# Agent attention into a top-1 mixture of experts: the second layer in 128 columns, gated out of its bank, single banks, another order of loads, left tiles by batch

## The chip, the cores and the metric

The kernel runs on one core of one Trainium2 chip. The metric is the device time of one execution in microseconds. A core has five engines that matter here, each working through its own list of instructions in order: PE (TensorE, matmuls, with its weight loads shown apart as PEld), DVE (VectorE), ACT (ScalarE), POOL (GpSimd) and SP (SyncE, which issues most of the DMA transfers). An engine that reaches an instruction whose operand is not there waits, and all that is queued behind it on that engine waits too.

## The reference

Four batches of N = 11456 tokens with C = 128 channels. The first function is agent attention (49 agents), the second a mixture of 8 experts with F = 1024 hidden units, of which each token takes the one with the largest logit.

```python
def _attn_ref(q, k, v, agents):
    scale = 1.0 / np.sqrt(q.shape[-1])
    def sm(a, b):                       # softmax of scale * a b^T
        ...
    a2k = sm(agents, k)
    agent_v = a2k @ v
    q2a = sm(q, agents)
    return (q2a @ agent_v).astype(np.float32)

def _moe_ref(x, w_gate, w_output_gate, w1, w2):
    logits = x @ w_gate
    e_idx = np.argmax(logits, axis=1)
    ...
    gate_w = probs[np.arange(N), e_idx]
    eom = 1.0 / (1.0 + np.exp(-(x @ w_output_gate)))
    for e in range(E):
        mask = e_idx == e
        ...
        h = np.maximum(x[mask] @ w1[e], 0.0)
        ye = h @ w2[e]
        out[mask] = gate_w[mask, None] * eom[mask, e, None] * ye
```

## The kernel before

The tokens of a batch are cut into 12 units of 1024 (the last has 192). A unit of k passes `k_unit` (scores tile ks, copied to S, maximum mx), a unit of v passes `v_unit` (exponentials ev, sums av), and a unit of q passes `q_unit` (scores qs) and `q_rest`, which makes the softmax over the agents in two 16-bit parts, turns it by a DMA into x1 (tile x_ld in the profile), and computes gate logits lg and the tests t. What the attention gives for a token is a mix of 49 agent vectors, so that x @ w1 is x1 times a small matrix made once per batch.

This matrix is made by a chain of steps between the batches. `fold(b)` sums the agents' values (av from sel); `choose` finds the expert that most tokens of the batch take and loads its w1 and w2; `units`, `split_units`, `signs`, `linear` and `second` build the weights of the first layer (tiles awp, kr, pm, wp), those of the part that is linear (lin) and those of the second layer (vp, vv); `gates` builds those of the logits. Each of these is a few small operations on PE, DVE, ACT and POOL in turn. Hidden units whose sign is the same for all tokens of the batch go into lin, so that NK = 2 blocks of 128 hidden units remain.

The main stream (`main_stream`) has 92 tiles, 23 per batch, of four token tiles of 128 tokens each (the last of a batch has two of 96). `mm1` makes h = x1 times the first layer in a pair of banks of 2 x 512 columns of PSUM; `relu` makes the high 16-bit part hh on ACT and the low one hl on DVE; `mm2` makes y for one token tile from five matmuls: x1 with lin (256 columns: 128 with the high part of the weights, 128 with the low part), and for each of the two blocks hh with vv (256 columns) and hl with the high part of vv (128 columns). The columns of high and low parts stand side by side, so that two token tiles fill a bank. `finish` copies a bank to ys on ACT (ring of two), adds the two halves into os on POOL (ring of four), and `store` multiplies os by the gate factor of the tokens, smt, and sends it out. The factor smt is made by `route` for a group of three units at once, that is for six main tiles.

Tokens whose expert is not the batch's are left to a second path: `q_tail` counts them, `left_table` makes a table of tiles of up to 128 tokens of one expert, `left_index` computes indices and gathers the rows (tile big), and `left_static` computes each such tile with the expert's whole weights (let, lx, lh, ly) and `left_scatter` writes its rows over those of the main stream. PHASES names the batches of a table and the tiles that are computed in any case: batches 0 to 2 have one table with 16 tiles, batch 3 one with 3. A loop at the end, on a count read on the chip, covers what that does not hold; its body does not run with these inputs.

The order of all instructions is made when the kernel is built. The class Clock keeps an estimate of the time at which each engine gets to each instruction; `spawn` adds a generator with a priority to a list; `tick`, `block` and `idle` are called by the main stream between its matmuls, and each steps those generators whose next instruction would not have to wait by that estimate. `order()` is a list of all k, v and q units and says in which order they are loaded (SP issues) and scored; `AHEAD` bounds how many q units may be ahead of the main stream, `RING` how many tiles of hh and hl there are. PSUM has eight banks: four stand as two pairs for h and t, four are single.

## Time and profile before

| | |
|---|---|
| median of three runs (lowest to highest) | 931.98 us (928.88 to 932.38) |
| the profiled execution, its span, the rest | 932.74 us, 930.9 us, 1.8 us |
| mean granted clock of TensorE | 0.828 |
| busy over the span: PE, PEld, DVE, ACT, POOL | 76%, 58%, 64%, 44%, 45% |
| startup, until the first h | 83.4 us |
| main tiles of batch 0, 1, 2, 3 | 148.6, 133.9, 130.0, 170.8 us |
| between them | 61.4, 51.3, 48.4 us |
| after the last y | 103.1 us |

The stages were cut where the first h and the last y of each batch stand in PE's timeline. A row of stages gives, for each stretch, the busy time of each engine with its number of instructions, the clock that TensorE was granted as a share of 2.4 GHz, the busy share of the DMA engines and what they moved. A row of a group gives what an operation writes and reads, its shape, how often it ran, its busy time and the mean of one, and then the idle time of its engine just before it and who ended it. Matmuls overlap, so their own durations say little; the distance from one start to the next is what a matmul takes of PE.

### The profile page before, as it was taken

The page shows a single profiled execution, that of the slowest core. Times are in us where ns is not written, and L with a number is a line of the kernel's source. Part 1 is how long each engine was busy: PE and PEld are TensorE (multiplying, and loading weights), DVE is VectorE, ACT ScalarE, POOL GpSimd, SP SyncE. Part 2 cuts the span into 40 slices and gives each one's busy share as a digit, 9 for nine tenths or more (in the row PEclk, how much of TensorE's full clock was granted, in tenths as well). Part 3 has the DMA queues.
Part 4 walks back from the last instruction along what each step waited for, and adds up shares of the span by engine and source line. Part 5 has one row for each costly group of instructions (what it writes and reads, how often), then busy time and mean ns, then how long its engine had stood idle before and what let it go on. Part 6 is the DMA issues. An engine that isn't in the chain of part 4 may idle for free. (4 is left out here: it accounts for less than half of the span.)

```text
span 930.9 us, 22198 instructions
## 1 busy us (share of the span) xinstructions
PE 705.7 (76%) x8709; PEld 537.6 (58%) x8709; DVE 597.5 (64%) x1346; ACT 412.0 (44%) x836; POOL 415.1 (45%) x658
## 2 busy tenths in 40 slices
PE   9989768778637986968579869653876859898765
PEld 7777636556525754747456647451544637677654
DVE  2666678676745975867659868688784668663310
ACT  2353626454342653635435636444343435452221
POOL 3110427756300475655104956651237555673331
PEclk9999978997757977977579879775887869898787
DMA  9962565565951447749914577482004715549440
GB/s 326 314 225 72 175 118 168 145 196 163 282 151 39 142 153 188 199 132 211 263 52 139 166 197 206 139 251 46 7 20 149 146 53 160 168 148 297 138 134 27
DMA packets 105081, 146.75 MB, mean 158 GB/s; under 512 B 60477, under 2 KB 69425, under 8 KB 104972
## 3 DMA queue, kind: packets, MB, share of 16 engines
q1 hardware_dynamic: 103148, 143.18, 53.0%
q0 software_dynamic: 1824, 2.11, 1.1%
q8 instruction: 69, 1.13, 0.5%
q14 instruction: 40, 0.33, 0.1%
HBM read 96.79 MB, written 35.50 MB: 142 GB/s over the span
## 5 line engine op out<-in xcount | busy, mean ns | idle before, releaser
L223 POOL TENSOR_TENSOR os<-ys 128x256 f32<-128x256 f32 x180 | 133.8, 753 | 161.6 <-ACT ys L223 114.4
L223 PE MATMUL y<-vv,hh 128*128 128x256 f16 x720 | 180.7, 292 | 0.0
L223 PEld LDWEIGHTS <-x_ld 128*128 128x128 f16 (+1 forms) x1080 | 96.8, 108 | 106.0 <-issue 49.1
L223 ACT COPY ys<-y 128x512 f32<-128x512 f32 x180 | 103.7, 585 | 121.1 <-POOL os L223 66.1
L223 PE MATMUL y<-lin,x_ld 128*128 128x256 f16 x360 | 105.6, 293 | 64.6 <-ACT ys L223 44.0
L223 PE MATMUL y<-vv,hl 128*128 128x128 f16 x720 | 152.1, 231 | 0.0
L223 DVE SCALAR_TENSOR_TENSOR hl<-h,hh 128x1024 f16<-128x1024 f32 (+1 forms) x92 | 108.7, 1189 | 40.7 <-ACT hh L223 40.0
L223 ACT ACTIVATE hh<-h 128x1024 f16<-128x1024 f32 (+1 forms) x92 | 91.7, 1000 | 87.8 <-PE h L223 86.1
L223 DVE TENSOR_REDUCE tm<-t 128x4 f32<-128x1024 f32 (+1 forms) x92 | 108.8, 1196 | 32.4 <-PE t L223 31.3
L223 PE MATMUL h<-x_ld,w 128*128 128x512 f16 (+3 forms) x368 | 94.4, 398 | 14.3 <-DVE tm L223 5.5
L223 PEld LDWEIGHTS <-hh 128*128 128x128 f16 x720 | 75.2, 104 | 51.0 <-issue 44.5
L223 PE MATMUL t<-w,x_ld 128*128 128x256 f16 x360 | 77.4, 310 | 6.4 <-DVE hl L223 3.6
L223 PEld LDWEIGHTS <-hl 128*128 128x128 f16 x720 | 75.7, 105 | 6.9
L223 DVE TENSOR_TENSOR os<-os,smt 128x512 f32<-128x512 f32 (+1 forms) x61 | 44.9, 751 | 32.4 <-POOL os L223 27.6
L223 PE MATMUL ks<-at,k_ld 128*64 128x50 f32 (+1 forms) x1636 | 57.7, 233 | 4.1 <-DVE r L223 1.4
L223 PE MATMUL av<-v_ld,ev 128*64 128x129 f32 x720 | 51.2, 286 | 12.6 <-ACT ys L223 12.3
L223 PEld LDWEIGHTS ks<-at,k_ld 128*64 128x64 f32 (+1 forms) x1636 | 51.0, 143 | 12.0 <-issue 4.4
L223 PEld LDWEIGHTS <-w 128*128 128x128 f16 (+1 forms) x368 | 24.7, 96 | 56.6 <-issue 54.4
L223 PE MATMUL lh<-lxs,lw_ld 128*128 128x128 f32 x304 | 54.0, 310 | 4.1 <-ACT lxs L223 2.1
L223 PE MATMUL lg<-gs,x_ld 128*128 128x36 f16 x360 | 31.0, 192 | 33.6 <-DMA x_ld<-e 28.8
L223 PE MATMUL qs<-at,q_ld 128*32 128x50 f32 (+1 forms) x2124 | 50.7, 222 | 3.3 <-issue 2.1
L223 PEld LDWEIGHTS av<-v_ld,ev 128*64 128x64 f32 x720 | 40.5, 140 | 21.0 <-ACT ys L223 14.0
(292 smaller groups left out, 1380.2 us busy)
## 6 DMA issues: line engine op xcount, KB each, us to landing
v_ld<-v SPq DMA_DIRECT2D x44, 516.0 KB
q_ld<-qT SPq DMA_DIRECT2D x44, 512.0 KB
out<-os SPq DMA_DIRECT2D x88, 256.0 KB
k_ld<-kT SPq DMA_DIRECT2D x43, 512.0 KB
lw_ld<-w SPq DMA_DIRECT2D x38, 512.0 KB
efd<-ef SPq DMA_DIRECT2D x44, 200.0 KB
w1t<-w SPq DMA_DIRECT2D x4, 512.0 KB
w2t<-w SPq DMA_DIRECT2D x4, 512.0 KB
```

The source lines that it names most:

```text
L223: return getattr(self.eng, op)(*a, **k)
```

## The change

Five things are changed together.

- `mm2` makes y of a token tile from eight matmuls of 128 columns instead of five: lin in its high part and, for the first 49 rows, in its low part; hh with both parts of vv one after the other; hl as before. All of them go to the same 128 columns, so high and low parts are summed in PSUM, and the four token tiles of a main tile stand in one bank.
- `finish` takes the bank straight to os. Where the factor smt is there (by the order), DVE multiplies it in, or ACT in four instructions of 128 columns; where it isn't, ACT copies and POOL multiplies later (`late`). Over the program DVE does this for 15 tiles, ACT with the factor for 32, and ACT without it for 45. The rings ys and the POOL additions are gone; os still has four places, and a tile waits until the tile four before it is stored.
- PSUM is eight single banks. h takes two, relu runs on each by itself (hh on ACT, hl in `low` on DVE), and the tests t are made for two token tiles at a time.
- `order()` loads k of batch b+2 from four units before the end of batch b and v of batch b+1 earlier in batch b; eight k units of batch 1 are scored before the first main tile instead of three. RING is 4 (was 5), AHEAD 7 (was 5), SMALL 10 (was 8), and `block` has no quiet time after a gather.
- PHASES has a table for each batch with 10, 6, 1 and 4 tiles; the tables, the gathers and the tiles run as generators beside the main stream, with whatever place is free (`left_home`).

```diff
-LARGE, SMALL, KEEP = 7, 8, 3
-PHASES = [(0, 3, 16, 384), (3, 1, 3, 128)]
+LARGE, SMALL, KEEP = 7, 10, 3
+PHASES = [(0, 1, 10, 128), (1, 1, 6, 128), (2, 1, 1, 128), (3, 1, 4, 128)]
...
-    PAIRS = 2
-    banks = [[True, None] for _ in range(6)]
+    banks = [[True, None] for _ in range(8)]
...
-        for h in range(0, nt, 4):
-            n = min(4, nt - h)
-            yield from wait_pair()
-            t = pair(f"t{b}_{u}_{h}")
+        for h in range(0, nt, 2):
+            n = min(2, nt - h)
+            yield from wait_free()
+            t = bank(f"t{b}_{u}_{h}")
             mark = hold()
...
+        rest = [("k", 1, u) for u in range(PRE, NU)]
+        for g in range(2, B * NU):
+            b, u = divmod(g, NU)
+            items.append(("q", b, u))
+            if b == 0 and rest:
+                items += rest[:2]
+                del rest[:2]
+            if u >= NU - LEAD:
+                kb, k0 = b + 2, 2 * (u - NU + LEAD)
             else:
-                items += qs
+                kb, k0 = b + 1, 2 * (LEAD + u)
+            if 1 < kb < B and k0 < NU:
+                items += [("k", kb, k0), ("k", kb, k0 + 1)]
+            v0 = 2 * (u - (6 - LEAD))
+            if b == 0:
+                v0 -= 2 * ((NU - PRE) // 2 + 2 - (6 - LEAD)) if PRE < NU else 0
+            if b + 1 < B and 0 <= v0 < NU:
+                items += [("v", b + 1, v0), ("v", b + 1, v0 + 1)]
...
-    PRE = 6
+    LEAD = 4
+    PRE = 8
...
-    MIX0 = [(2, 0)] + [(1, 0)] * 4 + [(0, 0)] + [(0, 2)] * 6
-    MIX = [(3, 0)] * 4 + [(0, 0)] + [(0, 2)] * 6 + [(0, 0)]
...
-    EARLY = 3
+    EARLY = 8
...
-    RING = 5
+    RING = 4
...
-        p = pair(f"h{i}")
-        mark = hold()
+        p = []
         for g in range(NK):
-            PE.matmul(p[:, g, 0:w], own_[:, g * P:(g + 1) * P], x1, start=True, stop=False)
+            p.append((bank(f"h{i}_{g}"), hold()))
+        for g in range(NK):
+            PE.matmul(p[g][0][:, 0:w], own_[:, g * P:(g + 1) * P], x1, start=True, stop=False)
...
-        spawn(relu(i, p, mark), 0)
...
+        for g, (x, mark) in enumerate(p):
+            yield from ACT.q.activation(hh[:, g, 0:w], x[:, 0:w], AF.Relu)
+            spawn(low(x, hh[:, g, 0:w], hl[:, g, 0:w], mark, i), 0)
+
+    cut = [0] * NT
+
+    def low(x, hh, hl, mark, i):
+        yield from DVE.q.scalar_tensor_tensor(hl, x[:, 0:hl.shape[1]], 0.0, hh, op0=ALU.max, op1=ALU.subtract)
+        release(mark)
+        cut[i] += 1
 
...
         b, u, h, pp, n = tiles[i]
-        k, j = t // 2, t % 2
-        if j == 0:
-            Y[i, k] = bank(f"y{i}_{k}"), hold()
+        if t == 0:
+            Y[i] = bank(f"y{i}"), hold()
         x1, lin = X1[b, u][0], state[b]["lin"]
         hh, hl = H[i] if t + 1 < n else H.pop(i)
         vv = state[b]["vv"]
-        y = Y[i, k][0][0:pp, j * 2 * C:(j + 1) * 2 * C]
+        y = Y[i][0][0:pp, t * C:(t + 1) * C]
         sl = slice(t * pp, (t + 1) * pp)
-        PE.matmul(y, x1[:, (4 * h + t) * pp:(4 * h + t + 1) * pp], lin, start=(j == 0), stop=False)
+        xs = x1[:, (4 * h + t) * pp:(4 * h + t + 1) * pp]
+        PE.matmul(y, xs, lin[:, 0:C], start=(t == 0), stop=False)
+        PE.matmul(y, xs[0:A], lin[0:A, C:2 * C], start=False, stop=False)
         tick()
         for g in range(NK):
-            PE.matmul(y, hh[:, g, sl], vv[:, g].rearrange("p h c -> p (h c)"), start=False, stop=False)
+            PE.matmul(y, hh[:, g, sl], vv[:, g, 0, :], start=False, stop=False)
+            PE.matmul(y, hh[:, g, sl], vv[:, g, 1, :], start=False, stop=False)
             tick()
-            PE.matmul(y[:, 0:C], hl[:, g, sl], vv[:, g, 0, :], start=False, stop=(g == NK - 1 and j == 1))
+            PE.matmul(y, hl[:, g, sl], vv[:, g, 0, :], start=False, stop=(g == NK - 1 and t == n - 1))
...
+        if t == n - 1:
+            if 4 * h + n == UNITS[u][2]:
+                scored(("x1", b, u))
+            spawn(finish(i), 0)
...
+    def finish(i):
         b, u, h, pp, n = tiles[i]
...
+        while i > 3 and i - 4 not in done or ended[0] < i:
+            yield None
+        os = wk.tile([P, 4, C], F32, name=f"os{i}", tag="os", bufs=4)
+        y, mark = Y.pop(i)
+        yv = y[0:pp, 0:n * C].rearrange("p (t c) -> p t c", c=C)
+        ended[0] = i + 1
+        if (b, u) not in SM:
+            yield from ACT.q.copy(os[0:pp, 0:n, :], yv)
+            release(mark)
+            spawn(late(i, os))
+            return
+        smt = SM[b, u][0:pp, 4 * h:4 * h + n]
+        if clk.vt["DVE"] <= clk.vt["ACT"]:
+            yield from DVE.q.tensor_tensor(os[0:pp, 0:n, :], yv, smt.unsqueeze(2).broadcast_to([pp, n, C]), op=ALU.mult)
+        else:
+            for t in range(n):
+                yield from ACT.q.activation(os[0:pp, t, :], yv[:, t, :], AF.Copy, scale=smt[:, t:t + 1])
+        release(mark)
+        yield from store(i, os)
...
+    def late(i, os):
+        b, u, h, pp, n = tiles[i]
+        while (b, u) not in SM:
+            yield None
+        smt = SM[b, u][0:pp, 4 * h:4 * h + n]
+        yield from POOL.q.tensor_tensor(os[0:pp, 0:n, :], os[0:pp, 0:n, :],
+                                        smt.unsqueeze(2).broadcast_to([pp, n, C]), op=ALU.mult)
+        yield from store(i, os)
...
-            if m1 < NT and m1 + 1 - freed <= RING and pair_free() is not None and pair_free()[0] <= now + 20.0:
+            if m1 < NT and m1 + 1 - freed <= RING and frees(2):
...
-            if i in H and "lin" in st and "vv" in st and clk.at([H[i][1], st["vv"], st["lin"]]) <= now:
-                can2 = t % 2 > 0 or n_free() > 0
+            if i in H and cut[i] == NK and "lin" in st and "vv" in st and clk.at([H[i][1], st["vv"], st["lin"]]) <= now:
+                can2 = t > 0 or n_free() > 0
...
+    left_todo = [(ph, k) for ph, x in enumerate(PHASES) for k in range(x[2])]
...
+    def left_tables():
+
+        for ph, (b0, nb, nst, _) in enumerate(PHASES):
+            while counted[0] < b0 + nb:
+                yield None
+            yield from left_table(ph)
...
+    def left_prepare():
+
+        for ph, (b0, nb, nst, _) in enumerate(PHASES):
+            while ph not in tables:
+                yield None
+            for i in range(0, nst, NSTM):
+                n = min(NSTM, nst - i)
+                while left_home() is None:
                     yield None
...
-    AHEAD = 5
+    AHEAD = 7
```

PE, batch 0: one token tile of the second layer, as far as its first block. `x10_..._ld` is the turned softmax, `lin0` and `vv0` are the weights of batch 0, the number behind y, hh and hl is that of the main tile. Before (tile 22):

```order
L223 LDWEIGHTS hl21_3567
L223 MATMUL y21_1_3665<-vv0_1560,hl21_3567 128x128
L223 LDWEIGHTS x10_11_ld_3363
L223 MATMUL y22_0_3686<-lin0_98,x10_11_ld_3363 96x256
L223 LDWEIGHTS hh22_3631
L223 MATMUL y22_0_3686<-vv0_1560,hh22_3631 96x256
```

After (tile 17):

```order
L217 LDWEIGHTS w0_1_1670
L217 MATMUL h18_1_3988<-x20_3_ld_3770,w0_1_1670 128x512
L217 LDWEIGHTS x10_8_ld_3219
L217 MATMUL y17_3907<-lin0_98,x10_8_ld_3219 128x128
L217 LDWEIGHTS x10_8_ld_3219
L217 MATMUL y17_3907<-lin0_98,x10_8_ld_3219 128x128
L217 LDWEIGHTS hh17_3805
L217 MATMUL y17_3907<-vv0_1744,hh17_3805 128x128
L217 LDWEIGHTS hh17_3805
L217 MATMUL y17_3907<-vv0_1744,hh17_3805 128x128
```

Each matmul of 256 columns has become two of 128 with a weight load of the same operand before each.

PE, from batch 0 to batch 1. `y22` is the last tile of batch 0, `av1_3804` from `sel` is the fold of batch 1, `qs`, `ks`, `av` with two numbers are units of scores and values, `ga1` the gates. Before:

```order
L223 MATMUL y22_0_3686<-vv0_1560,hh22_3631 96x256
L223 LDWEIGHTS hl22_3632
L223 MATMUL y22_0_3686<-vv0_1560,hl22_3632 96x128
L223 MATMUL qs1_1_3641<-at_74,q1_1_ld_3154 64x50 x16
L223 MATMUL av1_10_3719<-v1_10_ld_3214,ev1_10_3584 64x129 x8
L223 MATMUL av1_11_3735<-v1_11_ld_3262,ev1_11_3646 64x129 x2
L223 MATMUL qs1_2_3758<-at_74,q1_2_ld_3285 64x50 x16
L223 MATMUL ks2_0_3785<-at_74,k2_0_ld_3543 64x50 x16
L223 MATMUL av1_3804<-sel_72,avs1_0_2555 128x50 x2
L223 MATMUL ks2_1_3818<-at_74,k2_1_ld_3580 64x50 x16
L223 MATMUL ks2_2_3844<-at_74,k2_2_ld_3642 64x50 x16
```

After, at the first tiles that stand behind the fold's chain:

```order
L217 MATMUL y17_3907<-vv0_1744,hh17_3805 128x128
L217 LDWEIGHTS hl17_3806
L217 MATMUL y17_3907<-vv0_1744,hl17_3806 128x128
L217 LDWEIGHTS A161_3441
L217 MATMUL wp1_0_4040<-pm1_3499,A161_3441 128x512
L217 LDWEIGHTS A161_3441
L217 MATMUL wp1_0_4040<-pm1_3499,A161_3441 128x512
L217 LDWEIGHTS A161_3441
L217 MATMUL wp1_0_4040<-pm1_3499,A161_3441 128x512
L217 LDWEIGHTS A161_3441
L217 MATMUL wp1_0_4040<-pm1_3499,A161_3441 128x512
```

Before, the fold of batch 1 stands behind y22 and wp1 behind that; now wp1 stands between y17 and y18 of batch 0. The fold itself stands eight tiles earlier, ahead of y10; at the next two batches five (y29 to y33) and seven (y49 to y55) main tiles stand between fold and wp.

ACT, in batch 1: the eviction of tiles 33 and 34. `ev`, `qz`, `ld_`, `eo`, `S3` and `lv` belong to units of attention and gate logits. Before:

```order
L223 COPY avs2_0_5135<-av2_0_5136 128x129
L223 ACTIVATE qz1_6_4964<-ef1_6_4978 128x8x49
L223 ACTIVATE ev2_3_5259<-ev2_3_5259 128x400
L223 ACTIVATE ld_1_3_5213<-ld_1_3_5213 128x192
L223 ACTIVATE qz1_7_5153<-ef1_7_5175 128x8x49
L223 ACTIVATE eo1_3_5300<-ogs1_3_5296 128x24
L223 COPY ys33_0_5324<-y33_0_5214 128x512
L223 COPY ys33_1_5326<-y33_1_5231 128x512
```

After:

```order
L217 COPY lv_0_95<-lg1_7_6206 128x288
L217 ACTIVATE pm2_5866,less2_5865<-kr2_1_6068,nkey2_5848 128x512
L217 ACTIVATE eo1_3_6239<-ogs1_3_6188 128x24
L217 COPY lv_0_95<-lg1_8_6295 128x288
L217 ACTIVATE os33_6345<-y33_6233,smt1_3_6318 128x128 x4
L217 ACTIVATE v162_6354<-w2t2_5549,s22_s_5762 128x4x128 x2
L217 CAST w2_0_6392<-wp2_0_6359 128x512
L217 COPY S3_3_6086<-ks3_4_6408 128x400
L217 ACTIVATE hh34_6450<-h34_0_6433 128x512
L217 ACTIVATE hh34_6450<-h34_1_6434 128x512
```

The two copies of a tile, with POOL's additions of os33 and os34 behind them, have become four multiplications by `smt1_3` straight into os33; `hh` of a tile is two rows instead of one.

## Rows read from the trace of the kernel before

**Rows 1.** Stages: stretch, length, busy of PE, PEld, DVE, ACT, POOL; clock, DMA, GB/s

```profile
0.00:83.40 83.40, 76.87 (x1071) 62.15 (x1071) 43.30 (x132) 30.45 (x73) 15.86 (x53) 0.98 0.72 242
83.40:232.00 148.60, 116.37 (x1745) 84.99 (x1742) 103.63 (x179) 75.73 (x141) 76.70 (x124) 0.87 0.58 162
232.00:293.40 61.40, 32.87 (x416) 25.39 (x416) 34.19 (x117) 21.10 (x53) 13.06 (x23) 0.61 0.61 165
293.40:427.30 133.90, 110.72 (x1587) 81.28 (x1586) 101.24 (x171) 70.45 (x129) 76.23 (x122) 0.87 0.56 163
427.30:478.60 51.30, 31.91 (x392) 26.06 (x392) 34.58 (x113) 21.10 (x54) 12.90 (x24) 0.60 0.74 177
478.60:608.60 130.00, 107.52 (x1587) 78.83 (x1585) 100.83 (x171) 70.27 (x129) 76.97 (x123) 0.89 0.57 168
608.60:657.00 48.40, 23.43 (x214) 17.70 (x213) 38.83 (x140) 18.83 (x50) 12.13 (x23) 0.61 0.50 122
657.00:827.80 170.80, 133.63 (x1252) 97.18 (x1249) 116.19 (x230) 76.34 (x144) 94.53 (x128) 0.84 0.39 109
827.80:930.90 103.10, 72.36 (x465) 64.01 (x465) 24.70 (x97) 27.68 (x67) 36.68 (x42) 0.82 0.47 146
sum 930.90, PE 705.66 PEld 537.58 DVE 597.49 ACT 411.95 POOL 415.06; mean PE 78.41 PEld 59.73 DVE 66.39 ACT 45.77 POOL 46.12
```

**Rows 2.** Timeline of PE, first boundary: start, duration, instruction, idle before

```profile
236.81 0.65 PE L223 MATMUL av<-sel,avs 128*128 128x50 f32 x4
...
282.98 1.01 PE L223 MATMUL wp<-pm,A 128*128 128x512 f16 x2 [10.73 <-DVE pm L223]
...
292.33 0.39 PE L223 MATMUL wp<-pm,R 128*128 128x256 f16 x2
```

**Rows 3.** Waits: engine, what waited, for what; total us, times, longest

```profile
PE y L223 <- ACT ys L223: 44.0, 16, 6.3
...
POOL os L223 <- DMA out<-os: 34.8, 11, 10.2
```

**Rows 4.** Groups by shape: operation, count, busy us, mean ns, idle before

```profile
L223 ACT COPY ys<-y 128x512 f32<-128x512 f32 x176 | 101.4, 585 | 121.1 <-POOL os L223 66.1 <-PE y L223 49.5 <-PE qs L223 2.1
...
L223 DVE TENSOR_TENSOR os<-os,smt 128x512 f32<-128x512 f32 x59 | 42.8, 740 | 28.1 <-POOL os L223 23.3 <-POOL smt L223 4.8
...
L223 DVE SCALAR_TENSOR_TENSOR hl<-h,hh 128x1024 f16<-128x1024 f32 x88 | 106.5, 1218 | 40.3 <-ACT hh L223 39.7 <-issue 0.2
L223 DVE SCALAR_TENSOR_TENSOR hl<-h,hh 128x384 f16<-128x384 f32 x4 | 2.2, 554 | 0.4 <-ACT hh L223 0.3
...
L223 DVE TENSOR_REDUCE tm<-t 128x4 f32<-128x1024 f32 x88 | 106.1, 1219 | 30.2 <-PE t L223 29.2 <-issue 0.8
```

**Rows 5.** Timeline of PE and PEld, one token tile and a run of loads

```profile
352.14 0.28 PE L223 MATMUL y<-lin,x_ld 128*128 128x256 f16 x1
...
352.37 0.22 PE L223 MATMUL y<-vv,hl 128*128 128x128 f16 x1
352.42 0.27 PE L223 MATMUL y<-vv,hh 128*128 128x256 f16 x1
...
352.59 0.27 PE L223 MATMUL y<-lin,x_ld 128*128 128x256 f16 x1
...
352.37 0.10 PEld L223 LDWEIGHTS <-hh 128*128 128x128 f16 x1
...
357.05 0.29 PEld L223 LDWEIGHTS <-x_ld 128*128 128x128 f16 x8 [2.45 <-DMA x_ld<-e]
```

**Rows 6.** The tail: stage of tile ly alone; a DVE step; two of the chain

```profile
827.80:930.90 103.10, 30.13 (x208) 28.36 (x208) 4.78 (x13) 0.82 0.47 146
...
862.11 0.17 DVE L223 TENSOR_TENSOR ppi<-pexc,tot 128x8 f32<-128x8 f32 x1 [1.31 <-PE lh L223]
...
902.30 0.43 PE let L223
...
921.58 0.71 POOL out L223
```

More of the change, by code (lines that the diff above doesn't have):

```diff
@@ L293, in agent_attention_top1_moe @@
     resting = [False]
-    others = list(range(6))
     def n_free():
-        return sum(banks[k][0] for k in others)
+        return sum(x[0] for x in banks)
     def when_free(x):
@@ L333, in idle_bank, with frees @@
         return min(free)[1] if len(free) > 1 and min(free)[0] <= clk.now() - 600.0 else None
-    def pair_free():
-        free = [(when_free(banks[k]), k) for k in range(PAIRS) if banks[k][0]]
-        return min(free) if free else None
-    def wait_pair():
-        while True:
-            x = pair_free()
-            if x is not None and x[0] <= clk.now() + 50.0:
-                return
-            yield None
+    def frees(n):
+        free = sorted(when_free(x) for x in banks if x[0])
+        return len(free) >= n and free[n - 1] <= clk.now() + 20.0
+    KEEP_LONG, KEEP_SHORT = 2, 1
     def wait_free(long=False):
@@ L416, in agent_attention_top1_moe @@
     e16s = []
-    for i in range(4):
+    for i in range(3):
         t = cp.tile([P, 8, P], F16, name=f"e16_{i}")
@@ L521, in block @@
     def block():
-        if clk.now() < clk.quiet:
-            return
         clk.slots = [0, 0, 2]
-        for x in list(streams):
-            if x[3] is not None and x[3][0] == "PE" and clk.can(x[3], x[0]):
-                step(x)
+        going = True
+        while going and clk.slots[2]:
+            going = False
+            for x in list(streams):
+                if x[3] is not None and x[3][0] == "PE" and clk.can(x[3], x[0]):
+                    step(x)
+                    going = True
     def blocked(o, pairs, last=None):
@@ L1353, in agent_attention_top1_moe @@
     OFF = 1.0
-    RING = 5
+    RING = 4
     H = {}
     Y = {}
-    done, summed = set(), set()
+    done = set()
     def mm1(i):
@@ new lines, in agent_attention_top1_moe, with left_home, got @@
+    SETS = ["left"] + [f"S{j}" for j in range(4)]
+    holds = {x: [] for x in SETS}
+    def left_home():
+        for x in SETS:
+            gone = x == "left" or B - 1 in K and K[B - 1]["v"] >= min(3 * int(x[1:]) + 3, NU)
+            if gone and all(y in stored for y in holds[x]):
+                return x
+        return None
+    def left_prepare():
[5 more added lines that the diff above has]
+                while left_home() is None:
+                    yield None
+                tag = left_home()
+                holds[tag] = [(ph, i + k) for k in range(n)]
+                big = wk.tile([P, NSTM * (NCOL + A2 + C)], F32, name=f"big{ph}_{i}", tag=tag, bufs=1)
+                def got(k, t, ti, tu, ef, oa, i=i, ph=ph):
+                    ready[ph, i + k] = t, ti, k, tu[:, k:k + 1], ef[:, k, :], oa[:, k, :]
+                yield from left_index(ph, i, n, f"s{ph}_{i}", got, big)
@@ L1796, in left_static @@
             yield None
-        todo = [(ph, k) for ph, x in enumerate(PHASES) for k in range(x[2])][way::WAYS]
         ops = {}
+        mine = []
         finished = [0]
         def fronts():
-            for i, (ph, k) in enumerate(todo):
-                while (ph, k) not in ready or i > finished[0]:
+            while left_todo:
+                while left_todo and (left_todo[0] not in ready or len(mine) > finished[0] + (way == 0)):
                     yield None
+                if not left_todo:
+                    return
+                ph, k = left_todo.pop(0)
+                mine.append((ph, k))
                 t, ti, kk, _, ef, _ = ready[ph, k]
@@ L1812, in left_static @@
         spawn(fronts(), LEFT - 1)
-        for ph, k in todo:
+        while left_todo or finished[0] < len(mine):
+            while finished[0] >= len(mine) and left_todo:
+                yield None
+            if finished[0] >= len(mine):
+                return
+            ph, k = mine[finished[0]]
             while (ph, k) not in ops:
```

116 lines of the change are left out of this document (28 added, 88 removed).

## The prediction, made before the changed kernel was run

> **What bounds the kernel now.** The profiled execution took 932.74 us, of which 930.9 are the span and 1.8 lie outside it; the median of the runs is 931.98, so sums made against 932.7 stand for the median to 0.1%. The first view is busy time by stage [rows 1], cut where the first and last matmul of the main stream (tiles h and y) of each batch stand. Its last line says that PE is busiest (705.66 of 930.90, 76%) and DVE next (597.49, 64%): no engine is the bound on average, and the place matters. The stages show a startup of 83.4 us with PE busy 92% of it, four batches of 148.6, 133.9, 130.0 and 170.8 (together 583.3), three boundaries between batches of 61.4, 51.3 and 48.4 (161.1) and a tail of 103.1. In a boundary PE is busy about half of the time and at a granted clock of 0.60 to 0.61 of 2.4 GHz, most of the time at the lower level of 1.2: no main tile stands there, because the next batch's weights come out of a chain of small steps. The second view, PE's timeline at the first boundary, gives that chain's ends [rows 2]: the fold (av from sel) starts at 236.81, the first wp at 282.98 after 10.73 us of waiting for DVE's pm, and the last wp ends at 292.33 + 0.39 = 292.72: 55.9 us. The waits [rows 3] show what costs inside batches: PE's y waited 44.0 us for ACT's copy ys, and POOL's os 34.8 us for the store of an earlier os. So the path runs through boundary chains, through the eviction inside batches, and through the tail.
>
> **The change, part by part.** Startup: six k units of batch 1 were loaded ahead, now eight, and eight instead of three are scored before the first h. PE is 92% busy there, with DMA at 0.72. What moves in is taken out of batch 0, so I take 0, with a tenth of the stage either way as bounds (-8 to +8), since no row separates the two.
>
> Boundaries: k loads of batch b+2 now start four units before the end of batch b, so the chain of the next batch is fed while main tiles are left; the order excerpt shows wp of batch 1 between y17 and y18, where before it stood behind y22. What stays of the 161.1 is the PE work in them: 32.87, 31.91 and 23.43 = 88.2 us at clock 0.61, or 53.6 at full clock. That is -107.5, bounds 0 (PE waits at the chain's steps wherever they stand) and -161 (that work fits into PE's idle time of the batches, 583.3 - 468.2 = 115 us). I take the middle since idle time there is needed for other things below.
>
> Cover of the chain: fold and wp have 8, 5 and 7 tiles between them. A tile takes 133.9 / 23 = 5.8 us, so the cover is 46, 29 and 41 us for a chain of 55.9: short by 9, 27 and 15, together 51. Other units are queued between these, which is cover too; I take +25, bounds 0 and +51, or more if the chain itself grows (the slower rival).
>
> Eviction: 176 copies ys of 585 ns, the POOL adds behind them and the gates of os (59 of them on DVE at 740) [rows 4] go. Now a tile leaves its bank in one step, gated by DVE (15) or ACT (32), or by an ungated ACT copy with a POOL gate later (45). The hi and lo sums meet in PSUM, so a tile needs one bank where it needed two, and y's wait of 44.0 for ys loses its cause. What is late next: the os ring is still four and the step waits until tile i-4 is stored, while the gate factor comes once per three units; that is the 34.8 of [rows 3]. A delayed eviction now keeps a bank, not ys, behind it on ACT or DVE: the next hh or hl. I take -30, bounds -44 and 0.
>
> mm2: five matmuls per token tile become eight of 128 columns, 1024 columns as before. One token tile starts 0.45 us after the other (352.14 and 352.59), and a 128-column matmul is followed after 0.05 us (352.37 and 352.42) [rows 5], so eight take the same 0.45. Weight loads go from 5 to 8 per token tile; the nearest row is eight loads in 0.29 us, 36 ns each, below the spacing. I take 0, bounds 0 and the rival's price below.
>
> DVE: hl and tm are split in two, 88 of 1218 and 88 of 1219 ns [rows 4] become 176 each. By slope between 1218 for 1024 columns and 554 for 384 a 512-column step costs 687, so a pair costs 156 more: 2 x 88 x 0.156 = +27. The gates of os that leave DVE (59 x 740 = 43.7) less 15 new ones at about the same price: -33 or so. Tables of left tiles are built four times instead of twice and index sets grow from 5 to 7: +22 by share of DVE's 24.7 in the tail stage, an estimate. Net +16, hidden as long as DVE is not the bound: in the main part it goes from 529.5 (the seven stages) to 545.5.
>
> Left tiles: 21 static ones instead of 19, of which four stand behind the last y where 13 stood: eleven more in the main part than the six there. One takes 72.36 / 13 = 5.6 us of PE at clock 0.82 (208 ly matmuls, 16 a tile, are 13 tiles [rows 6]), 4.6 at full clock: 50 us. PE is idle a fifth of the batches, so a part is covered: +30, bounds 0 and +50.
>
> Clock: it is 0.84 to 0.89 in the batches. Fewer low stretches could give 468.2 x (1 - 0.87 / 0.95) = 39 us. I take 0 and keep -39 as a bound, since DVE would stand at 82% by this sum already.
>
> Main part: 744.4 - 107.5 + 25 - 30 + 30 = 662.
>
> Tail: the last y, then counts, the table, the gather, then left tiles. It was 103.1. Now the table of batch 3 alone with four tiles stands there. The table's DVE step ppi is at 862.11 and the first let of the last tiles at 902.30, 40.2 us for table and gather, with ten other left tiles beside it, so I take 35; behind it stand left tiles, three of whose kind took 902.30 to 921.58, 19.3 us, and 9.3 from there to the end of the span [rows 6]. Four tiles by that price are 26. From the last y to the table I take 5, an estimate below the 34.3 (862.11 - 827.80) that other left tiles filled; with 35 for the table, 26 and 9.3 it is 75.3, bounds 65 (nothing ahead of the table, 30 for it) and 90.
>
> Sum: 83.4 + 662 + 75.3 + 1.8 = **823 us**.
>
> **The rivals.** *DVE becomes the bound.* DVE's share was 0.72 over the four batches, 0.78 in the best batch and 0.80 in the last boundary; the sum asks for 545.5 / 662 = 0.82. If it holds no more than 0.76 to 0.78, the main part is 700 to 718 and the time 861 to 879; I take 870. For it: every main tile passes DVE twice in order (hl, tm), and now the chain and the left tables stand among them. Against it: DVE's idle time in a batch (32.7 of 133.9 us) lies in stages in which PE itself waited for evictions.
>
> *The chain grows and PE stands at its steps.* The chain's steps on DVE ran in a stage where DVE was 0.56 busy (34.19 of 61.40); placed among main tiles at 0.82, it can grow by that ratio from 55.9 to 82 us. The cover is then short by 36, 53 and 41 = 130 instead of 25, and every main tile behind wp waits on PE, in order. That is 823 + 105 = 928. If y's wait moves to the store in full as well (+30), the time is 958, slower. With that it decides from a shortfall of 105 us on (the 25 taken, and the 110 of gain less 30), which is a chain of about 74 us. For it: DVE's pm already kept wp 10.73 us. Against: the planner sets priorities, and the tiles between cover most.
>
> *Weight loads set the pace of mm2.* A weight load's row shows 0.10 us; eight one after another are 0.80 per token tile against 0.45, x 360 token tiles = +126, or 949 at most. Against it: the 36 ns per load and the 0.05 us of [rows 5]. The Trainium skill ("TensorE: Matmul & The Clock Gate", Back-to-back issue gap) speaks against the change here: in a stream of load and matmul pairs it gives about 81 ns per 128-column matmul. By that, as an estimate, 8 x 81 instead of 8 x 56 ns would add 72 us and give 895. The trace's single 128-column matmuls, each with a load of its own, are followed after 50 ns, which does not agree; a run of eight such pairs it does not show.
>
> *More is won than summed:* the boundary work fits into idle time and the clock rises: below 755.
>
> **How the numbers follow.** The forecast, 755 to 860 around 823: 0.64. DVE the bound, 870: 0.17. Below 755: 0.08. The chain grows, 928 to 958: 0.07. Weight loads, 895 to 949: 0.04. The range takes the forecast's case and DVE's, 755 to 885, and leaves out 0.08 + 0.11. A measurement of this kernel can tell about 0.5% from no change. Below 927: 0.64 + 0.17 + 0.08 + 0.03 of the last two = 0.92; within 0.5%: 0.02; above: 0.06.
>
> **What would show it.** Right: no boundary stage left between y22 and h23 longer than 20 us, clock there above 0.8; y<-ys gone from the waits; four ly tiles behind the last y; a tail of 65 to 90 us; y matmuls starting 55 ns apart. Wrong: PE waiting at wp, lin or vp over 15 us (the chain); DVE over 0.80 busy with PE's h waiting for hl (DVE); PE's y waiting for os in place of ys by more than 30 us; y starts 80 ns apart or more (loads). The prediction fails most easily on the cover of the chain, the one term taken at the middle without a row of its own.

## The result and the profile of the changed kernel

The changed kernel takes 867.99 us (median of four runs, 860.35 to 871.57) against 930.43 (921.0 to 932.38) for the kernel before, measured again beside it: a ratio of 0.9337 with a 95% interval of 0.9247 to 0.9427. It is faster by 6.6%, inside the range of the forecast (755 to 885) and 45 us above its middle (823). Medians and ranges here are of all executions, and the ratios leave out those that ran in a slower state of the chip (below, the 819.0 of one kernel).

The profiled execution took 871.57 us with a span of 869.7. These are its stages, cut as in [rows 1]: startup, batch 0, what lies between, batch 1, 2 and 3, the tail, and then the whole main part from the first h to the last y. The columns are stretch, length, busy time of PE, PEld, DVE, ACT and POOL with their numbers of instructions, the granted clock, the DMA share and GB/s.

```profile
0.00:86.50 86.50, 80.85 (x1251) 66.86 (x1252) 44.38 (x138) 32.56 (x78) 15.64 (x53) 1.00 0.79 265
86.50:259.40 172.90, 154.54 (x2429) 110.78 (x2427) 120.63 (x307) 80.63 (x188) 55.88 (x97) 0.94 0.64 178
259.40:260.80 1.40, 0.89 (x15) 0.71 (x13) 1.15 (x5) 0.52 (x2) 0.83 (x1) 1.00 0.80 115
260.80:491.30 230.50, 204.96 (x2863) 146.54 (x2860) 159.88 (x430) 100.93 (x254) 93.91 (x155) 0.84 0.65 182
491.30:664.30 173.00, 164.57 (x2013) 122.49 (x2012) 131.14 (x394) 88.64 (x231) 66.80 (x104) 0.95 0.66 172
664.30:798.70 134.40, 130.34 (x1492) 96.57 (x1490) 88.95 (x248) 65.87 (x164) 51.50 (x81) 1.00 0.44 125
798.70:869.70 71.00, 27.16 (x149) 23.22 (x149) 13.67 (x62) 8.81 (x22) 12.38 (x13) 0.61 0.30 96
86.50:798.70 712.20, 655.31 (x8800) 477.09 (x8797) 501.74 (x1381) 336.59 (x835) 268.92 (x436) 0.92 0.61 168
```

The boundaries of 61.4, 51.3 and 48.4 us are gone: 1.4 us lie between batch 0 and batch 1, and at the other two the first h of a batch starts before the last y of the one ahead. The main part fell from 744.4 to 712.2 and the tail from 103.1 to 71.0. What is striking is PE: it is busy 92% of the main part (97% of batch 3), at a higher clock than before. DVE is busy 70% of it. So PE is now the engine to look at, though the change was meant to leave its columns as they were.

Where PE's time went shows in one token tile. This is PE's timeline in the changed kernel (start, duration, instruction), and under it three rows of PEld from its groups by shape (count, busy us, mean ns, idle time before them).

```profile
104.69 0.38 PE L217 MATMUL y<-lin,x_ld 128*128 128x128 f16 x2
105.00 0.28 PE L217 MATMUL y<-vv,hh 128*128 128x128 f16 x2
105.12 0.22 PE L217 MATMUL y<-vv,hl 128*128 128x128 f16 x1
105.17 0.27 PE L217 MATMUL y<-vv,hh 128*128 128x128 f16 x2
105.28 0.22 PE L217 MATMUL y<-vv,hl 128*128 128x128 f16 x1
105.34 0.92 PE L217 MATMUL h<-x_ld,w 128*128 128x512 f16 x4
```

```profile
L217 PEld LDWEIGHTS <-x_ld 128*128 128x128 f16 x1056 | 91.5, 102 | 42.9 <-issue 31.6 <-DVE avd L217 0.9 <-DMA x_ld<-e 0.5
...
L217 PEld LDWEIGHTS <-x_ld 49*128 49x128 f16 x352 | 32.8, 93 | 53.2 <-issue 26.0
...
L217 PEld LDWEIGHTS <-w 19*128 19x128 f16 x184 | 8.7, 91 | 39.6 <-issue 39.6
```

A token tile takes 104.69 to 105.34, 0.65 us, where [rows 5] has 0.45. The six matmuls of vv keep 56 ns each. The two of lin take 0.31 us (104.69 to 105.00) instead of 0.11. The second of them uses the first 49 rows of the array alone, and its weight load is the one with idle time before it: 53.2 us before 352 loads, while the 1056 full loads of x_ld have 42.9. Over all token tiles at full clock, the median from the first lin matmul to the second is 152 ns and from the second to the next matmul 159, together 311 where two plain 128-column matmuls take 112.

### The profile page after: what moved, and what is told of

It is laid out like the page before. It is cut to its first block, busy times and chain, and to the rows that moved or that the text cites. A ratio compares the mean times of both kernels' runs of the same rounds, so it can differ in the third digit from the quotient of the medians.

```text
span 869.7 us, 25317 instructions
## 1 busy us (share of the span) xinstructions
PE 763.3 (88%) x10197; PEld 567.2 (65%) x10197; DVE 559.8 (64%) x1580; ACT 378.0 (43%) x935; POOL 296.9 (34%) x502
## 5 line engine op out<-in xcount | busy, mean ns | idle before, releaser
L217 PEld LDWEIGHTS <-x_ld 128*128 128x128 f16 (+3 forms) x1440 | 127.7, 101 | 97.3 <-issue 57.9
L217 PE MATMUL y<-vv,hh 128*128 128x128 f16 (+1 forms) x1440 | 183.4, 228 | 0.0
L217 PE MATMUL y<-lin,x_ld 128*128 128x128 f16 x720 | 141.0, 230 | 14.6 <-DVE tm L217 4.3
L217 DVE SCALAR_TENSOR_TENSOR hl<-h,hh 128x512 f16<-128x512 f32 (+1 forms) x184 | 116.5, 668 | 50.6 <-ACT hh L217 50.4
L217 DVE TENSOR_REDUCE tm<-t 128x2 f32<-128x512 f32 x180 | 119.2, 680 | 28.7 <-PE t L217 28.4
L217 PEld LDWEIGHTS <-hh 128*128 128x128 f16 (+1 forms) x1440 | 110.0, 102 | 21.0 <-issue 0.5
L217 ACT ACTIVATE hh<-h 128x512 f16<-128x512 f32 (+1 forms) x184 | 98.3, 589 | 50.5 <-PE h L217 49.2
L217 PE MATMUL ly<-lw_ld,lh 128*128 128x128 f32 x336 | 70.3, 316 | 0.0
L217 ACT ACTIVATE os<-y,smt 128x128 f32<-128x128 f32 x128 | 37.1, 369 | 54.1 <-PE y L217 25.2
L217 PEld LDWEIGHTS lh<-lxs,lw_ld 128*128 128x128 f32 x336 | 53.7, 210 | 5.5 <-issue 1.1
L217 PEld LDWEIGHTS ly<-lw_ld,lh 128*128 128x128 f32 x336 | 52.8, 207 | 3.1 <-issue 0.2
```

The source lines that it names most:

```text
L217: return getattr(self.eng, op)(*a, **k)
```

## The experiments

One fact is needed to read them: every edit is planned anew. The planner counts a matmul's columns in proportion to its rows when it estimates the clock of PE, so even the number of rows changes the order of all engines. Two pairs of kernels that differ only in 98 or 128 rows, with the same matmul spacing to 4 ns, measure 803.28 against 807.93 in one order of loads and 812.25 against 792.32 in the other. So up to about 20 us between two plans is scatter of the plan, far more than the scatter of the runs, and I take no smaller difference as the effect of an edit. Two pairs are few, so a difference not far above 20 us is weak evidence too. The runs were made in three groups; the kernel before, run again with each, took 928.71, 927.97 and 928.15 us, so times of different groups can be compared.

### All 128 rows for the low part of lin

```diff
-        PE.matmul(y, xs[0:A], lin[0:A, C:2 * C], start=False, stop=False)
+        PE.matmul(y, xs, lin[:, C:2 * C], start=False, stop=False)
```

> The changed kernel, but the low part of lin is multiplied over all 128 rows of the token tile (the rows behind the first 49 are zeros), so that every weight load of the second layer has 128 rows. Theory one, a load of 49 rows waits for the matmul before it and the next one waits again: the two lin matmuls of a token tile fall from 2 x 157 ns to 2 x 56, 360 x 0.2 = 72 us of PE at full clock, and as PE is 92% busy in the main part the time falls from 868 to 795 to 815. Theory two, the main part is bound by DVE as the prediction's first rival has it: the time stays above 855. Theory three, each of the eight loads costs something: lin falls to 2 x 81 ns only and the time to some 820.

Measured: 807.93 us (804.96 to 819.0), ratio to before 0.8703, interval 0.8638 to 0.8768. Its token tile, and its stages (startup, main part, tail):

```profile
105.24 0.28 PE L217 MATMUL y<-lin,x_ld 128*128 128x128 f16 x2
105.36 0.28 PE L217 MATMUL y<-vv,hh 128*128 128x128 f16 x2
105.47 0.22 PE L217 MATMUL y<-vv,hl 128*128 128x128 f16 x1
105.53 0.27 PE L217 MATMUL y<-vv,hh 128*128 128x128 f16 x2
105.64 0.22 PE L217 MATMUL y<-vv,hl 128*128 128x128 f16 x1
105.70 0.28 PE L217 MATMUL y<-lin,x_ld 128*128 128x128 f16 x2
```

```profile
0.00:87.20 87.20, 83.13 (x1250) 68.41 (x1251) 44.53 (x138) 32.77 (x78) 15.63 (x53) 0.96 0.77 263
87.20:733.76 646.56, 579.07 (x8692) 458.04 (x8689) 512.43 (x1380) 332.70 (x818) 270.09 (x432) 0.91 0.67 185
733.76:806.48 72.72, 27.22 (x149) 23.31 (x149) 13.24 (x61) 9.42 (x24) 17.05 (x23) 0.63 0.29 93
```

The lin pair takes 0.12 us (105.24 to 105.36) and the token tile 0.46. With 2.6 times as many rows in that matmul the kernel is 60 us faster. PE's busy time of the main part, each by its own clock, falls from 655.31 x 0.92 = 603 to 579.07 x 0.91 = 527: 76 us, against 72 expected (one hundredth of the clock is 6 us of this). Theory one holds. The main part fell 65.6 us with DVE at more work (512.43 us against 501.74), so DVE was not the bound (theory two), and the pair went to 2 x 56, not to 2 x 81 (theory three).

### 98 rows

```diff
-        PE.matmul(y, xs[0:A], lin[0:A, C:2 * C], start=False, stop=False)
+        PE.matmul(y, xs[0:98], lin[0:98, C:2 * C], start=False, stop=False)
```

> The changed kernel, but the low part of lin is multiplied over 98 rows instead of 49 (the added rows are zeros). If any load narrower than the array waits, the lin pair stays at some 2 x 157 ns and the time at 868. If only loads of half the rows or fewer wait, the pair falls to 2 x 56 ns and the time to that of the kernel with 128 rows, 795 to 815.

Measured: 803.28 us (798.49 to 805.52), ratio 0.8656, interval 0.8596 to 0.8716. The load of 98 rows does not wait:

```profile
L217 PEld LDWEIGHTS <-x_ld 98*128 98x128 f16 x352 | 35.6, 101 | 20.4 <-issue 19.6
```

Its idle time is 20.4 us against 53.2, and the medians around it are 56 and 60 ns. So it is not narrowness as such: 98 rows go through as 128 do, 49 do not. Nor is it 49 rows as such. In the changed kernel a matmul of the left tiles that also has 49 rows (lx) stands six times right behind the 49-row matmul of lin, and there it starts 66 ns after it (median, at full clock). Behind a lin matmul of 98 rows in this run it starts after 151 ns, and behind one of 128 rows in the run above after 149. The price comes with the change between 49 rows and 98 or 128.

### The kernel before with lin in two matmuls of 128 columns

```diff
-        PE.matmul(y, x1[:, ...], lin, start=(j == 0), stop=False)
+        PE.matmul(y[:, 0:C], xs, lin[:, 0:C], start=(j == 0), stop=False)
+        PE.matmul(y[:, C:2 * C], xs, lin[:, C:2 * C], start=False, stop=False)
```

> The kernel before, but its 256-column matmul of lin is made as two of 128 columns with a weight load of 128 rows each. If columns alone set the pace (the prediction's term of 0 for eight matmuls instead of five), 932 stays within 1%. If each load has a price of its own, 25 ns by a spacing of 81 or 100 ns by the load's own row, it is 360 times that, 9 to 36 us more.

Measured: 919.06 us (913.67 to 919.79), ratio 0.9899, interval 0.9833 to 0.9965. Neither theory expected a gain; it lies in the tail (80.8 us against 103.1 of [rows 1]) and is a matter of the plan. The main part is 747.8 us long against 744.4. That is 3 us more, of the 9 to 36 that a price per load would give, though 3 us are far within the scatter of plans. The trace is plainer: at full clock the two matmuls of lin start 56 ns apart and the next one 56 ns behind, 112 ns where the single one of 256 columns took 109 in the kernel before. Over 360 token tiles that is 1 us.

### The old order of loads

```diff
-    LEAD = 4
-    PRE = 8
+    PRE = 6
...
-    EARLY = 8
+    EARLY = 3
```

(with `order()` as in the kernel before, and 128 rows for lin)

> The changed kernel with 128 rows for lin, but with the order of loads of the kernel before (k of the next batch with its last q units, v behind them, six k units of batch 1 ahead, three scored early). If the order is what filled the boundaries, stretches of 30 to 50 us without a main tile come back at three places and the time is 60 to 110 us above that of the kernel with 128 rows. If single banks and the shorter eviction filled them, it is within 20 us of it.

Measured: 792.32 us (788.48 to 794.5), ratio 0.8540, interval 0.8483 to 0.8598. The kernel is 16 us faster than the same with the changed order, and the fastest of all that ran. Its main part and tail, and then the three stretches from the last y of a batch to the first h of the next:

```profile
84.60:724.71 640.11, 570.18 (x8809) 453.55 (x8806) 525.58 (x1405) 335.19 (x820) 275.32 (x442) 0.94 0.69 193
724.71:786.60 61.89, 25.05 (x144) 22.03 (x144) 9.55 (x43) 8.84 (x23) 12.29 (x13) 0.65 0.26 84
...
236.52:260.50 23.98, 14.88 (x242) 10.95 (x243) 17.43 (x55) 9.77 (x24) 10.70 (x17) 0.79 0.54 186
408.44:420.02 11.58, 10.53 (x135) 8.21 (x134) 11.02 (x21) 4.13 (x11) 7.87 (x13) 1.00 0.58 187
557.99:585.99 28.00, 21.16 (x214) 16.42 (x213) 25.94 (x73) 12.28 (x29) 16.99 (x25) 0.99 0.70 191
```

Stretches without a main tile did come back, of 24, 12 and 28 us: 64 in all, where [rows 1] has 161. The three kernels with the changed order have at most 1.8 us at any of these places, and each of the nine with the old order that ran has at least one of 21 us or more. So the changed order does close them. The time does not follow, for PE is not idle there: it is busy 62, 91 and 76% of them, at a clock of 0.79, 1.00 and 0.99, where in [rows 1] it was busy about half at 0.60 to 0.61. The fold of batch 1 starts at 194.8, 42 us ahead of the end of the last y of batch 0 (236.5), though the loads come in the order of the kernel before. So it was not the order that moved the fold ahead. The first theory has its stretches, but shorter and without their price; the second has its time, though the stretches are not filled.

### The old order of loads with 49 rows

The change with the old `order()`, PRE and EARLY alone.

> The changed kernel with the order of loads of the kernel before alone (the low part of lin over 49 rows, as in the change). If the loads of 49 rows cost their 72 us of PE in any order, it is 50 to 75 us above the 792 of the same kernel with 128 rows: 842 to 867. If the old order has idle time of PE at the boundaries that takes them up, it is less than 30 us above: below 822.

Measured: 889.97 us (883.59 to 894.37), ratio 0.9575, interval 0.9502 to 0.9649. That is 98 us above 128 rows in the same order of loads, more than the 50 to 75 expected.

```profile
84.30:819.90 735.60, 672.78 (x8800) 485.61 (x8797) 509.04 (x1379) 336.08 (x820) 282.67 (x449) 0.91 0.60 166
```

PE's part by clock is 672.78 x 0.91 = 612 against 570.18 x 0.94 = 536, again 76 us. So the price of 49 rows on PE is the same in both orders; the other 22 us lie in what else the new plan brought, a lower clock among it (0.91 against 0.94). The sign of the order's own effect turns with the rows: the changed order is 22 us faster with 49, 16 slower with 128 and 9 faster with 98. That is no effect of the order that these runs can tell from scatter.

### The old order with 98 rows

> The kernel with the old order of loads (792), with the low part of lin over 98 rows instead of 128. The wait of a narrow load was gone at 98 rows in the other order, so it should be gone here too: 785 to 797, and the switch before the first matmul of hh, 60 ns there, is 4 ns more than with 128 rows, 1.4 us in all. If row counts below 128 have some cost of their own it is 800 or more.

Measured: 812.25 us (810.92 to 818.27), ratio 0.8759, interval 0.8703 to 0.8816. It missed its expectation by 15 us, with the lin pair at 56 and 60 ns as expected. PE's work is that of 128 rows; the plan is another. This run is what the figure for scatter above rests on.

### Two tables of left tiles, as before

From here on the base is the kernel with 128 rows and the old order (792.32).

```diff
-PHASES = [(0, 1, 10, 128), (1, 1, 6, 128), (2, 1, 1, 128), (3, 1, 4, 128)]
+PHASES = [(0, 3, 16, 384), (3, 1, 3, 128)]
```

> The kernel with 128 rows for lin and the old order of loads (792), with the two tables of left tiles of the kernel before (batches 0 to 2 with 16 tiles, batch 3 with 3) in place of four. If left tiles fill the idle time at the boundaries, they now come after batch 2 is counted: two boundaries are empty again and batch 3 and the tail get longer, 40 to 80 us more. If they only change places with other idle time, less than 20 more.

Measured: 829.22 us (825.08 to 833.99), ratio 0.8939, interval 0.8871 to 0.9008: 37 us more, just below the 40 to 80 of the first theory.

```profile
84.70:690.30 605.60, 509.13 (x8282) 392.95 (x8280) 486.51 (x1204) 298.37 (x707) 236.97 (x394) 0.90 0.63 175
690.30:828.80 138.50, 99.27 (x617) 87.28 (x616) 34.05 (x142) 36.25 (x92) 55.16 (x63) 0.75 0.46 150
```

The main part, with 16 left tiles fewer, is 34.5 us shorter, and the tail, with 14 more, 76.6 longer. The boundaries did not empty further: 25, 13 and 5 us lie between the last y and the next first h, where the base has 24, 12 and 28. So the 37 us come from the tail and not from the boundaries, as the first theory had it. By these lengths a left tile costs 2.2 us in the main part and 5.5 in the tail; what tables and plan have in that, the runs do not separate.

### Six banks

```diff
-    banks = [[True, None] for _ in range(8)]
+    banks = [[True, None] for _ in range(6)]
...
-        return min((when_free(banks[k]), k) for k in range(8) if banks[k][0])
+        return min((when_free(banks[k]), k) for k in range(6) if banks[k][0])
```

> The kernel with 128 rows for lin and the old order of loads (792), with six single banks of PSUM instead of eight. If the two more banks are what lets scores and values of the next batch run beside the main tiles, so that the boundaries fill, the fold moves back behind the last tile of a batch and the time rises by 50 us or more (842 and up). If it is the shorter way of y out of its bank (one bank per tile, one step), six suffice and the time rises by less than 20.

Measured: 824.89 us (822.3 to 829.88), ratio 0.8914, interval 0.8854 to 0.8975: 33 us more, between the two theories. The fold of batch 1 (200.0) still stands 55 us ahead of the last y of batch 0 (254.9), so the theory that the banks moved it falls.

```profile
83.50:754.90 671.40, 588.37 (x8716) 463.27 (x8713) 528.13 (x1394) 340.13 (x849) 262.77 (x431) 0.93 0.66 184
```

All of it lies in the main part (671.4 against 640.1) with DVE at the same work. Two banks more seem to be worth some 30 us here, if two pairs measure the scatter well; what waits for them I did not pin down.

### Every tile gated later, on POOL

```diff
-        if (b, u) not in SM:
+        if True:
             yield from ACT.q.copy(os[0:pp, 0:n, :], yv)
```

> The kernel with 128 rows for lin and the old order of loads (792), but every tile leaves its bank by an ungated copy on ACT and is gated later on POOL; none is gated by DVE or ACT out of the bank. POOL gets 47 more of 1.05 us. If the gate in the step out of the bank is worth what the prediction took for eviction (30 us), the time rises by 20 to 40; if one bank per tile is the gain and the gate's place nothing, it stays within 8.

Measured: 804.78 us (803.25 to 805.68), ratio 0.8683, interval 0.8632 to 0.8734: 12 us more, between both expectations and within the scatter of plans. The gate's place is not shown to be worth anything.

### A shorter look ahead, a single pass per block, the early start

Three further edits to the same base: AHEAD 5 and SMALL 8 in place of 7 and 10; `block` with one pass over the streams; PRE 8 and EARLY 8.

> The kernel with 128 rows for lin and the old order of loads (792), with five q units and eight small places ahead (as before the change) in place of seven and ten. If it is the farther look ahead that let the scores and the fold of the next batch run beside main tiles, the fold moves back to within 15 us of the last tile of its batch and the time rises by 30 to 60. If banks and left tiles did that, the time stays within 12.

> The kernel with 128 rows for lin and the old order of loads (792), where a block steps each stream once, as before the change, rather than until nothing more can go. If two short runs of PE work in one block are what feeds the chain, 10 to 30 us more. If the tick between matmuls feeds it anyway, within 8.

> The kernel with 128 rows for lin and the old order of loads (792), with only the changed start: eight k units of batch 1 loaded ahead and eight scored before the first main tile. If the start is what costs the changed order its 16 us, this is 800 to 810. If the cost lies in k of batch b+2 and v of batch b+1 taking places and DMA time from q, it stays within 8 of 792.

Measured: 813.5 us (812.0 to 815.97; ratio 0.8746, interval 0.8699 to 0.8792), 795.9 (792.02 to 798.82; 0.8572, 0.8519 to 0.8626) and 798.39 (790.61 to 801.93; 0.8601, 0.8552 to 0.8651). The look ahead costs 21 us, at the edge of the scatter, and the fold stays 29 us ahead of the last y of batch 0 (208.8 and 238.0): not what moves it either. The other two make no difference that can be told.

## Why the prediction was right, and where it was wrong

The sign was right, and the measured time lies inside the range. It lies outside the 755 to 860 that the prediction gave its own case, though: the range reached 885 for the rival in which DVE is the bound, and the runs refute that rival. So it is partly luck that the range held: a term that the sum had at nothing came to nearly the time of a rival that was wrong. The miss lies in the main part, 712.2 us against 662; startup (86.5 against 83.4) and tail are within their bounds. By its own steps:

**mm2, taken at 0: wrong by 76 us of PE, 60 us of time.** This is the step that failed. It counted columns and weight loads, and its rows held loads of 128 rows only. The change's second lin matmul uses 49. A like price stood in the trace of before, in a row that the prediction did not look at:

```profile
L223 PEld LDWEIGHTS <-w 19*128 19x128 f16 x184 | 8.7, 91 | 38.3 <-issue 38.3
```

These are the 19-row matmuls of h; 184 loads had 38.3 us of idle time before them, 0.21 us each, and a 512-column matmul ahead of one took 311 ns to the next start instead of 216, and the y matmul behind them started after 317. So a change from 128 rows to 19 costs 95 ns there and the change back 101; from 128 to 49 it costs 152 - 56 = 96, and 159 - 56 = 103 back. With two such changes in each of 360 token tiles that is 72 us. The price of a change could be read in advance; that 49 rows would pay it as 19 do could not, since 98 do not. The rule also stood in the Trainium skill, "TensorEngine Tiling (Array Packing)", Key Properties: changing the tiling mode, not just the tile, drains TensorE; by its section Available Configurations the array is tiled in rows of 128, 64 or 32. The traces fit that: 49 rows wait behind 128, 98 do not. The page does not say in which mode a matmul of 49 or 98 rows runs, and gives no price. The 81 ns that the Trainium skill gives for a load and matmul pair ("TensorE: Matmul & The Clock Gate", Back-to-back issue gap), which the prediction weighed instead, is not borne out: runs of eight such pairs keep 56 ns.

With lin over 128 rows, which is the kernel that the sum in fact described, the time is 808 against 823 and the main part 646.6 against 662. That agreement is of the whole; some of its other terms are off too and offset each other.

**Boundaries and cover, -107.5 and +25: cause wrong in the main, size not measured.** The empty stretches went, but the larger part of them without the order of loads: with the old order 64 of the 161 us come back, and they cost no time that these runs can tell from scatter. What moved the fold ahead is not the order either. With the old order, and with that and the banks, the look ahead, the block passes or the tables undone one at a time, the fold still starts 29 us or more ahead of the batch's last y. What moves it is open; one bank for each tile of y, single banks for h and t, and `block` without its quiet time were undone in no run.

The chain did grow, as the slower rival said. Counted as the prediction's 55.9, from the fold to the end of the last wp, it is 68.0, 80.0 and 65.9 us for batches 1, 2 and 3, and the second is past the 74 from which that rival was to decide. It did not, for PE did not stand at wp: its idle time there fell, and none of it is for pm any more.

```profile
L223 PE MATMUL wp<-pm,A 128*128 128x512 f16 x32 | 13.1, 562 | 13.5 <-DVE pm L223 13.5
```

```profile
L217 PE MATMUL wp<-pm,A 128*128 128x512 f16 x32 | 10.7, 471 | 3.9 <-ACT os L217 2.0 <-DVE hl L217 1.9
```

So the +25 for a cover that is too short was not incurred: what is queued between the tiles covered the chain too. From fold to the first wp the rows are these, where [rows 2] has 46.2 us (now 59.3, 68.8 and 59.9; the third stretch is cut at 580.0):

```profile
166.20:225.50 59.30, 48.73 (x705) 32.53 (x702) 49.19 (x151) 30.78 (x76) 15.32 (x28) 0.94 0.69 172
315.70:384.50 68.80, 54.04 (x610) 36.43 (x609) 53.83 (x157) 28.19 (x73) 22.69 (x33) 0.68 0.50 131
520.80:580.00 59.20, 53.76 (x594) 38.57 (x592) 49.30 (x159) 33.94 (x90) 19.32 (x29) 0.91 0.58 160
```

PE is busy 82, 79 and 91% in these stretches. Only the second, the one with five tiles of cover, shows a clock below the others: 0.68 of 2.4 GHz, so a good part of it at the lower level of 1.2.

**Eviction, -30: the wait is gone, its worth in time not measured.** y's wait for ys of 44.0 us in [rows 3] is gone; what y waited for in PE's list now comes to 4.3 us at most for any one cause. What waits is ACT, for PE:

```profile
ACT os L217 <- PE y L217: 67.8, 41, 6.0
...
ACT os L217 <- DMA out<-os: 17.9, 5, 5.3
...
DVE os L217 <- DMA out<-os: 12.3, 3, 7.0
```

The wait for an earlier store is still there, 30.2 us on ACT and DVE where [rows 3] has 34.8 on POOL, but nothing on PE is behind it for long. How much of the gain is one bank for each tile the runs do not separate; that the gate in the step out of the bank has a part is not shown.

**Left tiles, +30, and the tail, 75.3.** The tail is 71.0, and its parts are near those forecast: 5.5 us to the table's step ppi (5 forecast), 28.4 from there to the first let (35), and 37.1 for four tiles and the end (35.3). A left tile in the main part costs 2.2 us by the run with two tables, where the forecast had 30 / 11 = 2.7.

**Clock, taken at 0: too small.** The main part went from 0.81 to 0.92 on average. This is the whole main part before:

```profile
83.40:827.80 744.40, 556.43 (x7177) 411.42 (x7174) 529.49 (x1118) 353.82 (x696) 362.52 (x564) 0.81 0.54 150
```

PE's 527 us by clock of the kernel with 128 rows would fill 651 us at 0.81, more than the 646.6 that the stage took; so the higher clock is a part of the gain, and its term belonged in the sum.

**DVE, 545.5 us: too high by 44, and no bound.** It was busy 501.74 us of the main part. The forecast added means of single instructions to a busy time. Added up one by one, DVE's instructions of the main part come to 592 us, against 590 before, but in the records they overlap by 91 us now and by 60 before, so that busy time fell. The rival at 870 gave the measured time almost exactly and is wrong all the same: with 128 rows DVE is busy 512.43 of 646.56 (79%) and with the old order 525.58 of 640.11 (82%), above the 0.78 at which the rival let it stop.

**What the gain is made of.** From 930 to the fastest kernel (792) it is 138 us. Above the scatter of 20 us stand only a table for each batch (37) and the two banks more (33); the look ahead (21) is at its edge. The rest is not taken apart.

## What to carry to other kernels

When a matmul is cut, compare the rows it uses with those of its neighbours, not only its columns: a change from 128 rows to 49 and back cost 0.2 us here, and the fewer rows saved nothing. A time that agrees with a rival does not confirm it; ask what its engine's busy share says, and change the one thing that it says is free. A stretch without main tiles is not yet lost time: read how busy the engine is in it, and at what clock. Where a planner lays out the whole program, edits that do the same work differed by 20 us in 800 here, so one comparison of two plans settles nothing below that.

## What the runs showed of the hardware that was not expected

One of DVE's small two-input steps ran far longer beside two-input steps of POOL. In the kernel before, one such step at the end of batch 0 stands beside two of POOL's additions, and one in batch 1 beside a step of a unit (e):

```profile
231.67 1.42 DVE L223 TENSOR_TENSOR lr<-lr,rm 128x144 f32<-128x144 f32 x1
...
231.51 1.41 POOL L223 TENSOR_TENSOR os<-ys 128x256 f32<-128x256 f32 x2
...
322.47 1.02 DVE L223 TENSOR_TENSOR lr<-lr,rm 128x192 f32<-128x192 f32 x1
...
322.37 0.90 POOL L223 TENSOR_TENSOR e<-ef,e 128x392 f16<-128x392 f32 x1
```

The step occurs 16 times. Eight times a two-input step of POOL was running when it started: it took 785 to 1419 ns, and ended 0.17 to 0.23 us after a two-input step of POOL (of the eight, four stood beside additions, four beside steps e and ev). The other eight times it took 297 to 358 ns. After the change POOL was ahead of it only twice: once it took 565 ns, and once, with 0.06 us of POOL's step left, 291. Where POOL began second, twice, it took 342 and 348. The group with 192 columns, before and then after:

```profile
L223 DVE TENSOR_TENSOR lr<-lr,rm 128x192 f32<-128x192 f32 x12 | 8.5, 712 | 0.1
```

```profile
L217 DVE TENSOR_TENSOR lr<-lr,rm 128x192 f32<-128x192 f32 x12 | 4.2, 347 | 0.0
```

The same operation takes 712 ns on average before and 347 after, 4.3 us in all: a small part of why DVE's sum came out lower. The additions are gone, but steps e and ev are not; that these meet it so seldom now is a matter of the plan. The Trainium skill says it ("SBUF — State Buffer", Who interferes with whom): a DVE instruction with two inputs in SBUF contends with a GpSimd instruction that reads SBUF, and the order of issue decides which of the two blocks. The trace agrees, with the long steps behind a POOL step that began ahead of them. DVE's hl and tm of 1024 columns, which read PSUM, show no such difference: their means are 1.216 and 1.220 us beside POOL's additions and 1.218 both without.
